# Gates repeated over the partitions by matmuls, one DMA transposition per chunk, x moved by chunk, and a new order: one layer with sliding attention and a gated MLP

## The chip, the cores and the metric

The kernel runs on one core of one Trainium2 chip. The metric is the device time of an execution in microseconds (us); the kernel before is given as the median of three executions. The profile shows one more execution, whose own time is given beside its span (first to last instruction). Engines are named as in the profile: PE is TensorE, DVE is VectorE, ACT is ScalarE, POOL is GpSimd, SP is SyncE (here it only issues DMAs).

## The reference, cut to what matters

One transformer layer, conditioned by a vector c, over 2048 tokens of 640 features, in bfloat16:

```
mod = silu(c) @ w_mod                       # six vectors of 640: sa, ca, ga, sb, cb, gb
h = layernorm(x) * (1 + ca) + sa
q, k, v = split(h @ wqkv)                   # 32 heads of 20
p = softmax(q k^T / sqrt(20), causal, the last 256 keys only)
x = x + ga * ((p v) @ wo)                   # ga: the first gate
h = layernorm(x) * (1 + cb) + sb
x = x + gb * ((sigmoid(h @ w_gate) * (h @ w_up)) @ w_down)    # gb: the second gate; inner width 1536
```

## The kernel before, in words

**Tiling.** The tokens are cut into 8 chunks (`a`) of 256, each of two blocks (`bi`) of 128 tokens, one token per partition. The kernel first computes `mod` (lines 537 to 690), then for each chunk: layer norm 1 (`ln1`), projections (`qkv`), attention, output projection (`outproj`, with layer norm 2), MLP (`mlp`). Weights stay in SBUF; w_mod comes in pieces into the space that wd, wu and hh use later.

**The order is written out by hand.** Every step is an `Op` made by `P.op` (called `A`): engines that may run it, a function, what it reads and writes. `PLAN` (line 295) is a list of integers that gives the order and the engine of each: `code // 5` is the number of the operation in the order of its creation, `code % 5` is its engine in the list PE, ACT, DVE, POOL, SP. `SLOTS` gives, in the same order, which buffer of its pool each tile takes. `emit` writes each engine's instructions in that order, with semaphore waits for what an operation depends on. So each engine works strictly in order: an operation whose input is late holds up all behind it on its engine. That holds for SP too, which issues nearly all DMAs. The costs and priorities in the calls are those of the planner that made `PLAN`; the kernel itself does not use them.

**mod.** `silubc` is silu(c). Five products on TensorE (tags modA, lines 673 to 683), one for each piece of w_mod, give sa and ca into `mA`, copied from PSUM by DVE at line 685. Before and between them stand matmuls on zeros ("warm", `zeros`, line 589; `HEAT` and `REHEAT` count them). The other four vectors come from `mod_tiles` (line 632): a product that leaves the 640 values of a gate as four rows of 160, on the partition groups 0, 32, 64 and 96. `mod_gate` (line 652) scales them into `grow`, writes the four rows to DRAM, and reads them back as one row of 640, repeated over the 128 partitions, into `gbc`. wo (line 1153) and wd (line 1090) are then multiplied by `gbc`, the gate folded into the weight.

**Layer norm and transposition.** `ln_stats` computes mean and variance of each block on DVE (line 700), the power -1/2 on POOL (706, 708), and the normalised block on DVE or POOL (721, 718). The product needs features on the partitions. For chunks 0 and 1 TensorE transposes (`by_block`, `pe_transposes`); for the others, and always for the MLP's input h2T, a DMA transposition from SBUF to SBUF, issued on SP (`transp_dma`, line 728), one per block. `modulate` (line 737) then applies (1 + c) and s to the transposed tile, feature by feature, on DVE, ACT or POOL.

**Projections and attention.** Q and K are evicted to `stg` in groups of 32 columns per head and transposed by DMA per block (by TensorE for chunk 0). A score set (line 916) is 8 or 16 matmuls into four PSUM banks (tile S); ACT takes the exp of the whole set in one instruction (line 943), POOL masks it (951, 953), and the PV product follows (`burst`). There are 6 sets for chunk 0 and 12 for each other chunk, 90 in all. S has one buffer, so the next set waits for the exp. Between the sets, `PLAN` puts projections of later chunks and MLP work of earlier ones on TensorE (all through `mm`, lines 605 and 606, called from `pe_chain`). The projections and the MLP use the pool M of four PSUM banks.

**Loads and stores.** x is loaded in blocks of 128 tokens, once for layer norm 1 (`p_x0`; the first three chunks keep it, `p_x1`) and once more for the residual of the later chunks. The result is stored per block, from SP or ACT.

Of the kernel before, what the change touches and what calls it, by code (L numbers as in the profile page):

```python
# [72 lines left out]

class Op:
# [4 lines left out]
class Prog:  # L79
# [8 lines left out]
    def op(self, eng, fn, dur, reads=(), writes=(), prio=50.0, lat=0.05, work=None, tmin=0.0, extra=(), tag="", hold=(),  # L88
# [41 lines left out]
        for t in hold:  # L130
            tiles[t] = 1
# [159 lines left out]
def c_pe(n):  # L291
# [121 lines left out]
PQ = ()  # L413
KEEP = 3
DSAFE = 1.0
NPB = 0
OUTE = ("sp", "act")
XE = ("sp", "act")
MW = 64
AFTER = 1  # L420
NOW = 1
LEAD = 2
HEAT = (5, 1, 1, 1)
REHEAT = (2, 1, 1, 1, 2)
WSE = (("dve", "pool"), ("dve", "pool"))
# [782 lines left out]
```

## Time and profile before

| | us |
|---|---|
| median of three executions | 332.96 (332.66 to 333.0) |
| the profiled execution's own time | 332.18 |
| its span | 330.4 |
| busy: PE, ACT, DVE, POOL | 320.4, 231.6, 197.9, 180.9 |
| mean granted clock of TensorE | 0.995 |

How to read it: a row of the timeline gives the start, the time that it covers, the engine, the line, the operation with its tiles (out<-in) and a count; brackets give the idle time of the engine before it and what ended it. SPq is a DMA issue on SP: its time is that of the issue, not of the transfer. Groups by line add up busy time (us) and give the mean of one in ns. A row of windows gives, after the stretch and its length, the busy time of PE, PEld (weight loads), DVE, ACT and POOL with their counts, then the granted clock of TensorE as a share of full speed, the DMA engines' share, and GB/s. Matmuls are pipelined, so the time between two starts is the price of one, not its busy time.

### The profile page before, as it was taken

What the parts mean: (1) busy time and instruction counts of PE and PEld (TensorE: products, weight loads), DVE (VectorE), ACT (ScalarE), POOL (GpSimd) and SP (SyncE); (2) the same over time, 40 slices, a digit from 0 to 9 for tenths busy, and PEclk for the clock granted to TensorE, in tenths of its full rate; (3) what the DMA queues carried; (4) which work ended last, traced back from release to release, by engine and by line L of the source; (5) the groups of instructions that cost most, each with busy time, mean ns of one, the idle gap of its engine ahead of it and who ended that gap; (6) DMA issues with size and microseconds to landing.
All of it is one profiled execution on the core that took longest, in us unless ns stands there. A gap on an engine that the chain in (4) does not pass through costs nothing.

```text
span 330.4 us, 9903 instructions
## 1 busy us (share of the span) xinstructions
PE 320.4 (97%) x4115; PEld 228.0 (69%) x4115; DVE 197.9 (60%) x421; ACT 231.6 (70%) x225; POOL 180.9 (55%) x278
## 2 busy tenths in 40 slices
PE   6999999889999999999999999999999999999997
PEld 2676656556676777666776676776776777788885
DVE  4497789466785667665636552565546463584423
ACT  2599788797887787868897977787895777412220
POOL 3246859676768856748573674647382738401000
PEclk9899999999999999999999999999999999999999
DMA  7989999989900662224600500190120002003101
GB/s 236 365 285 219 200 223 190 245 195 284 265 15 13 139 105 40 58 43 108 114 2 22 93 2 2 50 152 17 43 62 22 22 22 62 4 18 59 62 3 41
DMA packets 65719, 33.87 MB, mean 103 GB/s; under 512 B 49930, under 2 KB 64138, under 8 KB 65674
## 3 DMA queue, kind: packets, MB, share of 16 engines
q1 hardware_dynamic: 64368, 31.77, 43.0%
q10 hardware_dynamic: 1306, 1.48, 1.6%
q8 instruction: 32, 0.52, 0.7%
q14 instruction: 13, 0.11, 0.1%
HBM read 18.68 MB, written 2.62 MB: 64 GB/s over the span
## 4 chain that ended last, share of the span: by engine, by line
PE 78%; DMA 9%; POOL 4%; ACT 3%; issue 2%; DVE 2%; SPq 1%; ACTq 0%; POOLq 0%; DVEq 0%
PE M L605 64%; PE S L606 7%; PE M L606 6%; DMA hT<-x 3%; ACT E L943 3%; DMA wu<-in_B_w_up_dram 2%; DMA wd<-in_B_w_down_dram 2%; DMA wd<-in_w_mod_dram 2%; SPq L508 1%; POOL E L951 1%; POOL E L953 1%; POOL hT L737 1%; PE S L605 1%; POOL st L708 0%; DVE hT L757 0%
## 5 line engine op out<-in xcount | busy, mean ns | idle before, releaser
L943 ACT ACTIVATE E<-S 128x2048 bf16<-128x2048 f32 x90 | 168.9, 1877 | 38.8 <-PE S L606 35.8
L951 POOL TENSOR_SCALAR_AFFINE_SELECT E<-E 128x512 bf16<-128x512 bf16 (+2 forms) x90 | 74.2, 836 | 37.6 <-ACT E L943 17.8
L953 POOL TENSOR_SCALAR_AFFINE_SELECT E<-E 128x512 bf16<-128x512 bf16 (+1 forms) x84 | 65.1, 786 | 28.2 <-ACT E L943 13.6
L605 PE MATMUL M<-h2T,wu 128*128 128x256 bf16 x480 | 75.5, 273 | 0.1
L605 PE MATMUL M<-h2T,wg 128*128 128x256 bf16 x480 | 73.7, 273 | 0.0
L605 PE MATMUL M<-wd,hh 128*128 128x320 bf16 (+2 forms) x396 | 59.8, 295 | 0.0
L1109 DVE SCALAR_TENSOR_TENSOR hh<-sig,M 128x512 bf16<-128x512 f32 x48 | 32.3, 677 | 35.7 <-ACT sig L1107 19.0
L605 PEld LDWEIGHTS M<-h2T,wu 128*128 128x128 bf16 x480 | 44.6, 98 | 11.4 <-issue 3.0
L605 PEld LDWEIGHTS M<-h2T,wg 128*128 128x128 bf16 x480 | 45.1, 98 | 9.7 <-issue 1.9
L1107 ACT ACTIVATE sig<-M 128x512 f32<-128x512 f32 x48 | 28.6, 596 | 31.8 <-PE M L605 27.5
L605 PEld LDWEIGHTS M<-wd,hh 128*128 128x128 bf16 x396 | 37.0, 98 | 14.5 <-issue 1.5
L606 PE MATMUL S<-QT,KT 20*128 20x256 bf16 (+1 forms) x960 | 35.9, 245 | 2.3 <-ACT E L943 2.1
L700 DVE BATCH_NORM_STATS2 st<-x 128x6 f32<-128x320 bf16 x64 | 29.1, 476 | 1.3 <-DMA x<-in_A_x_dram 1.0
L605 PE MATMUL M<-wq,hT 128*128 128x320 bf16 x160 | 29.1, 300 | 0.7 <-DVE stg L823 0.4
L606 PEld LDWEIGHTS S<-QT,KT 20*128 20x128 bf16 x960 | 14.1, 92 | 22.1 <-ACT E L943 12.5
L989 DVE STREAM_TRANSPOSE T<-M 128x512 f32<-128x512 f32 x32 | 21.9, 702 | 11.1 <-PE S L606 8.8
L605 PE MATMUL M<-wo,oT 128*128 128x320 bf16 x160 | 28.4, 300 | 0.0
L605 PE MATMUL M<-wv,hT 128*128 128x320 bf16 x160 | 28.3, 299 | 0.1
L605 PE MATMUL M<-wk,hT 128*128 128x320 bf16 x160 | 27.0, 299 | 1.0 <-POOL hT L737 1.0
L1128 DVE TENSOR_TENSOR x<-M,x 128x320 bf16<-128x320 f32 (+2 forms) x33 | 15.6, 476 | 19.9 <-PE M L605 19.5
L823 DVE CAST stg<-M 128x320 bf16<-128x320 f32 x37 | 17.7, 480 | 13.4 <-PE M L605 13.0
L1062 DVE TENSOR_TENSOR x<-M,x 128x320 bf16<-128x320 f32 x32 | 15.3, 484 | 13.7 <-PE M L605 11.6
(78 smaller groups left out, 300.8 us busy)
## 6 DMA issues: line engine op xcount, KB each, us to landing
x<-in_A_x_dram SPq DMA_DIRECT2D x21, 160.0 KB, 3.2
wd<-in_w_mod_dram SPq DMA_DIRECT2D x6, 320.0 KB, 5.1
wd<-in_B_w_down_dram SPq DMA_DIRECT2D x4, 480.0 KB, 6.1
out_dram<-x SPq DMA_DIRECT2D x11, 160.0 KB, 2.0
wu<-in_w_mod_dram SPq DMA_DIRECT2D x5, 320.0 KB, 6.9
wu<-in_B_w_up_dram SPq DMA_DIRECT2D x2, 576.0 KB, 7.7
wg<-in_B_w_gate_dram SPq DMA_DIRECT2D x2, 576.0 KB, 4.6
wq<-in_A_wqkv_dram SPq DMA_DIRECT2D x2, 400.0 KB, 7.6
```

The lines of the kernel that those rows point to most:

```text
L605: return e.matmul(o, l, r, start=st, stop=sp, skip_group_check=True)
L606: return e.matmul(o, l, r, start=st, stop=sp, tile_position=tp, skip_group_check=True)
L700: A("dve", lambda e, g, bi=bi, j=j: e.bn_stats(v(bi * 12 + j * 6, 6), src[bi].ap[:, j * 320:(j + 1) * 320]), 0.48, reads=[src[bi].r()], wr ...
L823: return e.tensor_copy(dst(), src())
L943: A("act", lambda e, eng: e.activation(E.ap[:], Sp.ap[:], ACT.Exp, scale=SM_SCALE), 1.876, reads=[Sp.r()], writes=[E.r()], prio=3, tag=f"e ...
L951: return e.affine_select(ap, ap, pattern=[[0, ap.shape[1]], [1, 128]], compare_op=ALU.is_ge, fill=0.0, base=0, channel_multiplier=-1)
L953: return e.affine_select(ap, ap, pattern=[[0, ap.shape[1]], [-1, 128]], compare_op=ALU.is_ge, fill=0.0, base=-1, channel_multiplier=1)
L989: A("dve", lambda e, g, h=h: e.transpose(T1.ap[:, 512 * h:512 * h + 512], X[h].ap), 0.694, reads=[X[h].r()], writes=[T1.r(h)], prio=3.5, t ...
L1062: A("dve", lambda e, g, ps=ps, bi=bi, half=half: e.tensor_tensor(x1[bi].ap[:, half * 320:half * 320 + 320], ps.ap[:, 0:320], x1[bi].ap[:, ...
L1107: A("act", lambda e, g, pg=pg, sg=sg: e.activation(sg.ap[:], pg.ap[:], ACT.Tanh, scale=0.5), c_act(512), reads=[pg.r()], writes=[sg.r()], ...
L1109: A("dve", lambda e, g, pu=pu, sg=sg, f0=f0: e.scalar_tensor_tensor(out=hh.ap[:, f0:f0 + 2, :], in0=sg.ap[:].rearrange("p (a b) -> p a b", ...
L1128: A("dve", lambda e, g, ps=ps, bi=bi, c0=c0, n=n: e.tensor_tensor(x1[bi].ap[:, c0:c0 + n], ps.ap[:, 0:n], x1[bi].ap[:, c0:c0 + n], op=ALU. ...
```

## The change

- **Gates.** `mod_gate` no longer goes through DRAM: four matmuls multiply a column of the identity matrix, repeated 128 times, with `grow`, which repeats each of the four rows over all partitions in PSUM; two evictions copy the halves to `gbc`.
- **Layout by chunk.** x0, x2, x1, hT, h2T, stg, QT and KT become tiles of a whole chunk with the block as an outer index ([128, 2, ...]); `Half` is the view of one block. Operands that spanned 256 contiguous columns are now two runs of 128.
- **One DMA transposition per chunk** for hT and h2T, instead of two. Q and K keep one per block (`QM` is empty).
- **x loaded, and the result stored, by chunk** (x of chunk 0 and the last chunk's result still by block); the second part of w_mod in two DMAs instead of five (`WM1`).
- **A new PLAN and new SLOTS.** PLAN has 1978 operations instead of 2012; SP has 92 instead of 128, ACT 220 instead of 234, DVE 440 instead of 421, POOL 261 instead of 266.

The new order at the start: SP issues x of chunk 1, x of chunk 0, the five pieces of w_mod for modA, wq, wk, x of chunk 2, wv, x of chunk 3, one part of wo, w_mod's second part and w_gate's first, and then the transposition hT of chunk 2. DVE does the statistics and normalisation of chunks 0 and 1 before it copies mA. On TensorE the heating matmuls stand in a row behind the transposition of c, a transposition of chunk 0 stands before the first modA product and two more before the third; two transpositions of chunk 1 come before the first projection.

```diff
+class Half:
+    def __init__(self, tile, bi):
+        self.tile = tile
+        self.bi = bi
+    def r(self, key=None):
+        return self.tile.r(("b", self.bi, key))
+    @property
+    def ap(self):
+        return self.tile.ap[:, self.bi, :]
...
+WM1 = (3, 5)
+QM = ()
...
-    p_x0 = sbpool("x0", 4, [128, D])
-    p_x2 = sbpool("x2", 2, [128, D])
-    p_x1 = sbpool("x1", 6, [128, D])
-    p_hT = sbpool("hT", 2, [128, NDT, CH])
-    p_h2 = sbpool("h2T", 2, [128, NDT, CH])
-    p_stg = sbpool("stg", 4, [128, 1024])
-    p_QT = sbpool("QT", 3, [128, NG, CH])
-    p_KT = sbpool("KT", 4, [128, NG, CH])
+    p_x0 = sbpool("x0", 2, [128, 2, D])
+    p_x2 = sbpool("x2", 1, [128, 2, D])
+    p_x1 = sbpool("x1", 3, [128, 2, D])
+    p_hT = sbpool("hT", 2, [128, 2, NDT, 128])
+    p_h2 = sbpool("h2T", 2, [128, 2, NDT, 128])
+    p_stg = sbpool("stg", 2, [128, 2, 1024])
+    p_QT = sbpool("QT", 3, [128, 2, NG, 128])
+    p_KT = sbpool("KT", 4, [128, 2, NG, 128])
...
-    def mod_gate(ps, n, factor, prio):
-        g = dram(f"gate{prio}", [4, 160])
-        Rd = R("gdram")
+    def mod_gate(ps, n, factor):
         A("dve", lambda e, _: e.tensor_scalar(grow[:], ps.ap[:, n * 160:n * 160 + 160], factor, None, op0=ALU.mult),
           c_dve(160), reads=[ps.r()], writes=[R_grow], prio=8, tag="grow")
-        dma(lambda: g, lambda: grow[0:128:32, :], 0.05, reads=[R_grow], writes=[Rd], prio=1, tag="gout", dur=0.42)
-        dma(lambda: gbc[:], lambda: g.rearrange("(o a) b -> o (a b)", o=1).to_broadcast([128, D]), 0.45, reads=[Rd], writes=[R_gbc],
-            prio=1, tag="gin", dlat=2.6)
+        gs = [Tile(p_M, "gb") for _ in range(2)]
+        def fn(e, g):
+            for j in range(4):
+                ins = mm(e, gs[j // 2].ap[:, j % 2 * 160:j % 2 * 160 + 160], ident[:, 32 * j:32 * j + 1].to_broadcast([128, 128]), grow[:],
+                         True, True)
+            return ins
+        A("pe", fn, 0.3, reads=[R_grow, R_ident], writes=[t.r() for t in gs], prio=8, lat=0.2, tag="gb", mode=0)
+        for h in range(2):
+            evac(lambda h=h: gbc[:, 320 * h:320 * h + 320], lambda t=gs[h]: t.ap[:, 0:320], 320, [gs[h].r()], [R_gbc[h]], 8, "gbe")
...
-                ap = dst.ap[:, dt, :]
+                ap = dst.ap[:, :, dt, :]
...
-            turned[a] = [transp_dma(lambda bi=bi: t.ap[:, :, bi * 128:(bi + 1) * 128], lambda bi=bi: src[bi].ap[:], 4, 0.29,
-                                    [src[bi].r()], [t.r(("t", bi))], 1.42, f"atr{a}") for bi in range(2)]
+            turned[a] = [transp_dma(lambda: flat3(t), lambda: flat(xt), 4, 0.58, [s.r() for s in src], [t.r("t")], 1.35, f"atr{a}")]
...
-            for bi in range(2):
-                transp_dma(lambda bi=bi: h2.ap[:, :, bi * 128:(bi + 1) * 128], lambda bi=bi: x2[bi].ap[:], 2, 0.29,
-                           [x2[bi].r()], [h2.r(("t", bi))], 1.42, f"btr{a}")
+            transp_dma(lambda: flat3(h2), lambda: flat(x2t), 2, 0.58, [x.r() for x in x2], [h2.r("t")], 1.35, f"btr{a}")
...
+            if a < NCH - 1:
+                if bi == 1:
+                    stored[a] = [dma(lambda: out_flat[2 * a * 128:(2 * a + 2) * 128, :].rearrange("(b p) d -> p b d", p=128), lambda: x1[0].tile.ap[:], 0.84,
+                                     reads=[x.r() for x in x1], prio=10, tag="out", dur=0.45, eng=OUTE)]
```

More of the change, by code (lines that the diff above doesn't have):

```diff
@@ L630, in pe_chain, with evac @@
         return o
+    def evac(dst, src, n, reads, writes, prio, tag):
+        def fn(e, g):
+            if g == "act":
+                return e.activation(dst(), src(), ACT.Copy)
+            return e.tensor_copy(dst(), src())
+        return A(("act", "dve"), fn, {"act": c_act(n), "dve": c_dve(n)}, reads=reads, writes=writes, prio=prio, tag=tag)
     def mod_tiles(parts, prio):
@@ L737, in mo @@
                 return e.tensor_scalar(ap, ap, sc[:, dt:dt + 1], sh[:, dt:dt + 1], op0=ALU.mult, op1=ALU.add)
-            A(MOE, mo, {"dve": 0.34, "act": 0.59, "pool": 0.55}, port=True, reads=[dst.r(("t", bi)) for bi in range(2)] + Rmod, writes=[dst.r(dt)], prio=prio, tag=f"{ln}modu{a}")
+            A(MOE, mo, {"dve": 0.34, "act": 0.59, "pool": 0.55}, port=True, reads=[dst.r("t")] + Rmod, writes=[dst.r(dt)], prio=prio, tag=f"{ln}modu{a}")
     def pe_transposes(src, dst, sc, sh, Rmod, prio, a, ln="a"):
@@ L1046, in outproj @@
         if a < KEEP:
-            x1 = [keep[2 * a], keep[2 * a + 1]]
+            x1 = keep[a]
         else:
-            x1 = [load_x(p_x1, 2 * a + bi, 15, eng=XE, extra=stored.get(a - 3, ())) for bi in range(2)]
+            x1 = load_x(p_x1, a, 15, eng=XE, extra=stored.get(a - 3, ()), tag="y")
         for bi in range(2):
@@ L1067, in outproj @@
                 add_pair(x1[bi], pss, 4.5, f"res1_{a}")
-        x2 = [Tile(p_x2, f"x2_{2 * a + bi}") for bi in range(2)]
+        x2t = Tile(p_x2, f"x2_{a}")
+        x2 = [Half(x2t, bi) for bi in range(2)]
         ln_stats(x1, x2, 7, "b", a)
```

133 lines of the change are left out of this document (69 added, 64 removed), and 208 rows, old and new, of the table PLAN.

## The prediction

> **What bounds the kernel now.** The page comes first: span, engine shares, bytes per slice, the chain that ended last.
>
> ```profile
> span 330.4 us, 9903 instructions
> PE 320.4 (97%) x4115; PEld 228.0 (69%) x4115; DVE 197.9 (60%) x421; ACT 231.6 (70%) x225; POOL 180.9 (55%) x278
> GB/s 236 365 285 219 200 223 190 245 195 284 265 15 13 139 105 40 58 43 108 114 2 22 93 2 2 50 152 17 43 62 22 22 22 62 4 18 59 62 3 41
> PE 78%; DMA 9%; POOL 4%; ACT 3%; issue 2%; DVE 2%; SPq 1%; ACTq 0%; POOLq 0%; DVEq 0%
> ```
>
> TensorE is bound almost throughout, so a change off its queue pays only where TensorE waits. The DMA engines carry 190 to 365 GB/s in the first eleven slices of 8.26 us (to 91 us) and little afterwards. DMA, POOL and ACT stand in the chain at the front; late in the kernel it is TensorE. The change is decided before 91 us.
>
> Next the timeline of TensorE, for unit prices.
>
> ```profile
> 12.64 3.09 PE L605 MATMUL M<-wq,hT 128*128 128x320 bf16 x20 [0.33 <-POOL hT L782]
> ...
> 29.67 0.87 PE L606 MATMUL M<-wu,silubc 128*32 128x160 bf16 x40
> ...
> 33.33 2.21 PE L605 MATMUL M<-wk,hT 128*128 128x320 bf16 x15 [1.01 <-POOL hT L737]
> ...
> 53.42 1.50 PE L606 MATMUL M<-E,V 128*32 128x256 bf16 x64
> 54.85 0.40 PE L606 MATMUL S<-QT,KT 20*128 20x256 bf16 x8
> ...
> 62.28 0.40 PE L606 MATMUL S<-QT,KT 20*128 20x256 bf16 x8
> 62.61 0.45 PE L605 MATMUL M<-wv,hT 128*128 128x320 bf16 x2
> 62.89 0.84 PE L605 MATMUL M<-wk,hT 128*128 128x320 bf16 x5
> 63.57 1.25 PE L605 MATMUL M<-wv,hT 128*128 128x320 bf16 x8
> 66.96 0.40 PE L606 MATMUL S<-QT,KT 20*128 20x128 bf16 x16 [2.14 <-ACT E L943]
> ```
>
> From start to start, five 320-column matmuls take 63.57 - 62.89 = 0.68 us, 0.136 each; a score set 62.61 - 62.28 = 0.33; a PV burst 54.85 - 53.42 = 1.43 (half that for chunk 0). Real projections begin at 12.64.
>
> Then ScalarE's timeline: each score set is followed by one exp.
>
> ```profile
> 19.61 1.88 ACT L943 ACTIVATE E<-S 128x2048 bf16<-128x2048 f32 x1 [0.21 <-PE S L606]
> ...
> 32.37 1.88 ACT L943 ACTIVATE E<-S 128x2048 bf16<-128x2048 f32 x1
> ...
> 36.15 1.88 ACT L943 ACTIVATE E<-S 128x2048 bf16<-128x2048 f32 x1 [0.54 <-PE S L606]
> ...
> 60.26 1.88 ACT L943 ACTIVATE E<-S 128x2048 bf16<-128x2048 f32 x1
> 64.44 0.60 ACT L736 ACTIVATE hT<-hT,mA 128x256 bf16<-128x256 bf16 x1 [2.31 <-DMA hT<-x]
> ...
> 65.05 1.85 ACT L943 ACTIVATE E<-S 128x2048 bf16<-128x2048 f32 x1
> ...
> 69.99 1.88 ACT L943 ACTIVATE E<-S 128x2048 bf16<-128x2048 f32 x1 [0.18 <-PE S L606]
> ```
>
> From the first exp (19.61) to that of chunk 2's first set (69.99) pass 50.4 us. The order list in the code puts there, on TensorE, 235 matmuls of 320 columns (235 x 0.136 = 32.0), 18 score sets (5.9), three PV bursts (0.7 + 0.7 + 1.4), two modulation products of at most 0.87 (1.7) and 28 identity products of 128 columns (by columns 0.055 each, 1.5): 43.9 us. The excess is 6.5. A set costs about 0.1 beyond its work even in an undisturbed stretch (32.37 to 36.15 apart), so 18 x 0.1 = 1.8 is ordinary and **4.7 us are stalls** that an order could avoid. Two are big: 36.15 - 32.37 = 3.78 where the order gives 15 matmuls and a set, 2.4 us with the 0.1 still out (1.3 lost: K of chunk 2 waited for hT); and 65.05 - 60.26 = 4.79 for the same 2.4 (2.3 lost: ScalarE, in order, sat before the modulation of hT of chunk 4, with two exps' work behind it, and TensorE waited 2.14 for the exp). The remaining 1.1 is spread thin. The second stall begins at a DMA transposition:
>
> ```profile
> 56.15 1.13 SPq L508 DMA_DIRECT2D wg<-in_B_w_gate_dram  x2
> 57.39 2.96 SPq L728 DMA_TRANSPOSE hT<-x  x2
> ```
>
> The pair was issued right behind two bulk loads of w_gate; its modulation could start at 64.44, 7 us after 57.39.
>
> **The change, part by part.** *Gates.* Rows by line and shape, then of the DMA view (median us to landing last).
>
> ```profile
> L605 PE MATMUL M<-ident,stg 128*128 128x128 bf16 x32 | 3.1, 219 | 0.0
> ...
> L1153 DVE TENSOR_TENSOR wo<-wo,gbc 128x640 bf16<-128x640 bf16 x5 | 2.1, 478 | 0.9 <-DMA gbc<-gate 0.9
> ...
> L655 DVE TENSOR_SCALAR grow<-M 128x160 bf16<-128x160 f32 x2 | 0.6, 296 | 0.0
> ```
>
> ```profile
> gbc<-gate SPq DMA_DIRECT2D x2, 160.0 KB, 5.1
> h2T<-x SPq DMA_TRANSPOSE x16, 2.6
> QT<-stg SPq DMA_TRANSPOSE x14, 3.4
> ```
>
> Removed: two DMAs per gate and a 5.1 us landing. Only 0.9 us of DVE idleness came from it, off the path. Added per gate: four matmuls of 160 columns, not in the trace; they lie between half of four 320-column ones (0.27) and four identity products of 128 columns with their drain (4 x 3.1/32 = 0.39). I take 0.27, since they stand in a row with other matmuls: 0.55 us for both gates. They lie on TensorE's own queue, with nothing to hide them. Two evictions of 320 columns, about as long as a scaling of wo (0.48), replace the landing; the order puts them on DVE, where they stand beside projections. The product waits for grow; behind it on TensorE stand chunk 1's V projections and the next score sets. grow follows the PV burst and the modulation product, both over a score set earlier, some 4 us of TensorE work, against 0.3 us on DVE and two PSUM transpositions ahead of it: no wait. Two of the four PSUM banks are held until the evictions: zero to 0.5, I take zero.
>
> *One transposition per chunk* (hT, h2T: 28 become 14).
>
> ```profile
> L728 SPq DMA_TRANSPOSE h2T<-x x16: 1199/1228/2100, 67.8 to 303.8; - x16
> L728 SPq DMA_TRANSPOSE QT<-stg x14: 1231/1264/3679, 27.5 to 220.1; - x14
> ```
>
> 640 columns cost SP 1.23 us and 1024 cost 1.26, so the issue hardly depends on size: 14 x 1.23 = 17 us less of SP time, all of it on a queue that ends nothing by itself. Landing: 2.6 us for 640 columns and 3.4 for 1024 gives about 3.9 for 1280; a pair of today lands 1.2 + 2.6 = 3.8 after its first issue (bounds: 2.6, as if size were free, and 2 x 2.6 = 5.2). So nothing is gained where both halves are ready, and where the second is late the merged one lands 1.3 later after it (2.6 to 3.9). Behind it on SP wait the next loads and q/k transpositions. After 91 us TensorE has work of other chunks to cover 1.3 us; before, it is in the stalls below. The two-run operands (2 x 128 columns) I price at nothing: the modulation product reads one of its weights in five runs of 32 columns and takes the same time per matmul.
>
> *Loads and stores by chunk* save SP issues of about 0.4 us each, again beside other work; a store then waits for the second half, which reuse of its buffer two chunks later covers.
>
> *The new order, head.* SP now issues chunk 1's x, then x of chunk 0, and only then w_mod; DVE does both chunks' statistics before it copies mA.
>
> ```profile
> 4.84 0.87 DVE L700 BATCH_NORM_STATS2 st<-x 128x6 f32<-128x320 bf16 x2
> ...
> 8.45 0.45 DVE L721 TENSOR_SCALAR x<-x,st 128x640 bf16<-128x640 bf16 x1 [1.02 <-POOL st L708]
> ...
> 11.69 0.17 DVE L685 COPY mA<-S 128x10 f32<-128x10 f32 x1 [2.79 <-PE S L605]
> ```
>
> ```profile
> 5.35 0.60 PE L592 MATMUL S<-E 128*128 128x512 bf16 x2
> ...
> 9.09 0.74 PE L605 MATMUL S<-silubc,wd 128*128 128x64 bf16 x10
> ...
> 10.05 0.74 PE L605 MATMUL S<-silubc,wd 128*128 128x64 bf16 x10
> ```
>
> ```profile
> 8.00:9.00 1.00, 1.00 (x14) 0.72 (x12) 0.45 (x1) 0.03 (x1) 0.41 (x1) 0.50 0.97 325
> ...
> 11.00:12.00 1.00, 1.00 (x18) 0.80 (x16) 0.31 (x3) 0.04 (x1) 0.00 (x0) 0.86 1.11 373
> ```
>
> DVE from 4.84: eight statistics (8 x 0.435), four aggregations (about 0.2), four normalisations (0.45), two memsets (0.2) make 6.5 us, so mA at 11.4, and with a wait for POOL's powers 11.9 instead of 11.69: **+0.2**. The w_mod pieces come 320 KB later, 1.0 us at the 325 GB/s of the window from 8 to 9, and TensorE waits longer than that for DVE. So TensorE is the question. Its first transposition now stands ahead of all five w_mod products and needs a normalisation that DVE reaches at about 7.9, and another one needed before the third product ends at 9.9. Today's products run at a granted clock of 0.50 (window 8 to 9), one with its reheating every 10.05 - 9.09 = 0.96 us. From 7.9 at that pace, with the transpositions, mA would come at 13.2: **+1.5**. But the new order runs its eight heating matmuls in one piece right before that point, where today they are done, in pieces, at 5.35 + 0.60 = 5.95 and TensorE then stands; those last two took 0.30 each, and half the clock came after the standstill. I take the full clock as granted: +0.2, and keep +1.5 as a rival.
>
> The Trainium skill, "TensorE: Matmul & The Clock Gate", section "Part 1: The HAM clock gate", says that the clock opens after a window of about 3.4 us of sustained work, and that the window runs freely. By that rule eight matmuls of heat just suffice, and run by run they may not; the 0.50 of the windows agrees with a gate of two states.
>
> *The new order, front.* Counted in the lists: up to chunk 2's first set TensorE has 5 projections fewer, and two transpositions have moved under the head (-0.2). K of chunk 2 comes after a score set more of other work, and no load blocks SP before hT of chunk 2: the 1.3 us stall goes. The wo scalings come earlier on DVE: half of the spread 1.1 goes. For chunk 4 the w_gate loads now stand behind hT. But the second K transposition of chunk 1, issued soon after that chunk's first exp (36.15 today), blocks SP till about 37, and behind it ten bulk loads, 4.2 MB, and five q/k and one hT transposition (1.6 MB) stand ahead of hT: 5.8 MB at the 223 to 245 GB/s of the busy slices after 40 us is 24 to 26 us, so it lands, itself included, at 62 to 65; at the bulk rate of 365 it would be 55. ScalarE reaches the modulation at about 60 (the exp before it, 60.26 today, comes some 1.5 earlier and lasts 1.88). I take 62, a stall of 2, and half of the spread waits: 2.6 of the 4.7 remain.
>
> **Sum.** One more wait counts, from the list of waits:
>
> ```profile
> PEld M L605 <- DMA wu<-in_B_w_up_dram: 0.4, 1, 0.4
> ```
>
> Against the profiled run (332.18; span 330.4, and 1.8 around it): +0.2 head, +0.55 gates, -0.2 transpositions moved, -4.7 + 2.6 stalls = -1.55, and -0.4 for the wait on the last w_up load after 80 us, which is issued some places earlier in the new order: about -2.0. The median of the runs shown, 332.96, lies 0.78 higher; against it, **331.0**.
>
> **Rivals.**
> 1. *The front runs clean*: hT of chunk 4 lands by 60, as the bulk rate would allow; stalls 0.6 instead of 2.6: 329.0. For it: SP issues fewer commands; against it: the bytes above.
> 2. *Cold head*: the clock is 0.5 during the w_mod products, +1.5 instead of +0.2: 332.3. For it, the 0.50 of the windows; against it, heat in one piece.
> 3. *The bulk holds hT of chunk 4* (slower): at 223 GB/s or less hT lands at 65; ScalarE stands 5 us before an exp and TensorE with it: +3 on the forecast, 334.0. It turns the sign from a landing of about 64 (331.0 + 2). For it: 7 us of latency today; against it: w_gate no longer stands before it and the gates' trip has gone.
> 4. *Nothing changes*: other waits take the place of those removed; 332.3 to 333.6. The forecast bets on half of them.
>
> **Chances.** About 0.2% (0.7 us) is what a measurement of this kernel can tell from no change. Forecast 0.40 (329.8 to 332.2), clean 0.18, cold 0.12 (half of it faster), slower 0.20, nothing 0.10. Faster 0.64, same 0.16, slower 0.20. The range leaves out half of the clean case's far side and of the slow one's: 328.3 to 334.2; the likeliest case's own is 329.8 to 332.2.
>
> **What would show it.** Head: first projection at 12.6 to 13.0 with a clock of 1.0 from 8 to 12 (14 and 0.5: rival 2). Front: exps of chunk 1's first set no more than 2.6 us behind the one before. ScalarE's wait before hT of chunk 4: about 2 us; none is rival 1, over 4 is rival 3. Gates: eight matmuls, under 0.6 us. Wrong altogether if TensorE's stalls after 91 us change, where I expect none.

## The result, and the profile after

The change made the kernel **slower by 0.67%**: 334.05 us (median of 15 executions, 332.32 to 335.54) against 332.04 for the kernel before, run beside it (15 executions, 330.1 to 333.0); ratio 1.0067, 95% interval 1.0042 to 1.0092. The forecast was 331.0. The profiled execution took 334.05 us, its span is 332.3 (before 330.4). Ratios here leave disturbed executions out, so they differ a little from the quotients of the medians.

The page of the changed kernel: span, engines, GB/s in 40 slices, the chain that ended last.

```profile
span 332.3 us, 9821 instructions
PE 320.7 (97%) x4123; PEld 229.0 (69%) x4123; DVE 201.8 (61%) x440; ACT 227.0 (68%) x215; POOL 183.0 (55%) x273
GB/s 233 370 373 141 221 248 214 202 216 290 166 62 36 8 73 136 3 82 80 121 49 2 38 5 2 41 145 0 73 113 2 41 2 42 41 0 65 17 41 39
PE 87%; DMA 9%; SPq 1%; ACT 1%; DVE 1%; issue 0%; DVEq 0%
```

The busy shares hardly differ from those before. What tells the two apart is ScalarE's timeline, the starts of the exps:

```profile
18.64 1.88 ACT L975 ACTIVATE E<-S 128x2048 bf16<-128x2048 f32 x1 [0.21 <-PE S L626]
...
31.18 1.88 ACT L975 ACTIVATE E<-S 128x2048 bf16<-128x2048 f32 x1
33.65 1.88 ACT L975 ACTIVATE E<-S 128x2048 bf16<-128x2048 f32 x1
...
55.10 1.88 ACT L975 ACTIVATE E<-S 128x2048 bf16<-128x2048 f32 x1 [0.51 <-PE S L626]
59.45 0.44 ACT L655 ACTIVATE stg<-M 128x320 bf16<-128x320 f32 x1 [2.47 <-PE M L625]
61.31 0.44 ACT L655 ACTIVATE stg<-M 128x320 bf16<-128x320 f32 x1 [1.43 <-PE M L625]
61.78 1.88 ACT L975 ACTIVATE E<-S 128x2048 bf16<-128x2048 f32 x1
63.55 0.59 ACT L768 ACTIVATE hT<-hT,mA 128x256 bf16<-128x256 bf16 x1
...
66.72 1.88 ACT L975 ACTIVATE E<-S 128x2048 bf16<-128x2048 f32 x1 [0.27 <-PE S L626]
...
71.39 1.88 ACT L975 ACTIVATE E<-S 128x2048 bf16<-128x2048 f32 x1 [2.69 <-PE S L626]
```

The first exp (the first score set of chunk 0) is 0.97 us earlier than in the profile before (19.61), and the stall in front of chunk 1's first set is gone (33.65 - 31.18 = 2.47, before 3.78). Then come two new ones, where the order gives a plain set of 2.5 us: 61.78 - 55.10 = 6.68 (**4.2 lost**) and 71.39 - 66.72 = 4.67 (**2.2 lost**). The stall of before at the modulation of hT of chunk 4 is gone: ScalarE comes to it at 63.55 without waiting. Over the span: -0.97 to the first exp, +3.69 from there to chunk 3's first exp (91.56 against 87.87; 1.2 of it is TensorE work that the order moved in there, by the prediction's unit prices), -0.82 after it, which makes +1.9 in all.

What ended the two new waits, from the chain of waits between 50 and 75 us (start, length, what):

```profile
50.47 5.91 DMA x<-in_A_x_dram
...
56.41 0.04 DVE st L732
...
57.29 0.63 DVE T L1021
...
57.97 3.31 PE M L625 x12
61.28 0.44 PE S L626 x8
...
61.78 7.35 DMA QT<-stg
...
69.22 1.79 PE M L625 x12
```

First wait: the load of chunk 5's x was issued at 50.47 and took 5.91 us. VectorE stood before chunk 5's statistics for it; behind those, in order, stood the turn of the PV result (T, line 1021) that frees a PSUM bank, and TensorE's next projection wanted that bank. Second wait: TensorE stood 2.03 us for Q3's transposition, though nobody wanted chunk 3's Q yet. The projection wanted was chunk 4's Q, and its staging buffer `stg` was still being read. (A projection reserves its staging buffer when it starts.) SP's timeline shows why both were late:

```profile
44.48 5.87 SPq L760 DMA_TRANSPOSE QT<-stg  x2
50.47 0.51 SPq L524 DMA_DIRECT2D x<-in_A_x_dram  x1
51.04 0.46 SPq L524 DMA_DIRECT2D wu<-in_B_w_up_dram  x1
51.66 5.87 SPq L760 DMA_TRANSPOSE KT<-stg  x2
57.64 1.36 SPq L760 DMA_TRANSPOSE hT<-x  x1
59.05 1.22 SPq L524 DMA_DIRECT2D wg<-in_B_w_gate_dram  x2
60.44 6.58 SPq L760 DMA_TRANSPOSE QT<-stg  x2
```

A transposition of Q or K is issued in 1.23 to 1.26 us when little is in flight; here two take 5.87 (Q2, and again K2) and 6.58 (Q3). Bulk loads stand in front of each pair; that they are the reason is tested below. Not every issue behind a load stretches: of K2's two the first takes 1.24 and the second 4.58, of Q3's 1.24 and 5.24. hT of chunk 3, behind four loads, took 9.7 us from issue to landing. All that follows on SP shifts with them. The Trainium skill, "Perfetto Trace Analysis", section "DMA Instruction — HWDGE (DVE, Sync)", says that the span shown of such an issue includes the wait for the descriptor generator and the writing of all descriptors, and that the DMA engines may begin early when these overfill the buffer. The rows agree with that reading: what stretches is the issue (5.24 us for one), not only the transfer.

The waits were 2.41 and 2.03 us, but the first one cost 4.2. TensorE's windows behind it (granted clock third from last):

```profile
58.00:60.00 2.00, 2.00 (x8) 1.13 (x9) 2.00 (x7) 0.44 (x1) 0.00 (x0) 0.52 1.23 253
60.00:62.00 2.00, 2.00 (x16) 0.87 (x15) 0.59 (x2) 0.66 (x2) 0.44 (x1) 0.63 1.02 183
```

The clock fell to half after the standstill: 4 us at 0.52 and 0.63 lose 1.7, and 2.4 + 1.7 is nearly all of the stall.

### The profile page after: what moved, and what is told of

Same layout as the page of the kernel before. It is cut to its first block, busy times and chain, and to the rows that moved or that the text cites. A ratio compares the mean times of both kernels' runs of the same rounds, so it can differ in the third digit from the quotient of the medians.

```text
span 332.3 us, 9821 instructions
## 1 busy us (share of the span) xinstructions
PE 320.7 (97%) x4123; PEld 229.0 (69%) x4123; DVE 201.8 (61%) x440; ACT 227.0 (68%) x215; POOL 183.0 (55%) x273
## 3 DMA queue, kind: packets, MB, share of 16 engines
HBM read 18.35 MB, written 2.62 MB: 63 GB/s over the span
## 4 chain that ended last, share of the span: by engine, by line
PE 87%; DMA 9%; SPq 1%; ACT 1%; DVE 1%; issue 0%; DVEq 0%
PE M L625 73%; PE S L626 8%; PE M L626 6%; DMA hT<-x 3%; DMA QT<-stg 2%; DMA wd<-in_w_mod_dram 2%; DMA x<-in_A_x_dram 2%; SPq L524 1%; ACT E L975 1%; SPq L760 0%; DVE T L1021 0%; ACT hT L768 0%; DVE hT L814 0%; DVE st L732 0%; PE S L625 0%
## 5 line engine op out<-in xcount | busy, mean ns | idle before, releaser
L985 POOL TENSOR_SCALAR_AFFINE_SELECT E<-E 128x512 bf16<-128x512 bf16 (+1 forms) x84 | 67.1, 809 | 47.2 <-ACT E L975 36.4
L625 PE MATMUL M<-h2T,wu 128*128 128x256 bf16 x480 | 74.3, 273 | 0.0
L625 PE MATMUL M<-h2T,wg 128*128 128x256 bf16 x480 | 72.9, 273 | 0.0
L625 PE MATMUL M<-wd,hh 128*128 128x320 bf16 (+2 forms) x396 | 60.5, 295 | 0.0
L625 PEld LDWEIGHTS M<-h2T,wu 128*128 128x128 bf16 x480 | 45.5, 98 | 9.7 <-issue 1.9
L656 DVE CAST stg<-M 128x320 bf16<-128x320 f32 x43 | 20.5, 482 | 17.4 <-PE M L625 17.2
L625 PE MATMUL M<-wv,hT 128*128 128x320 bf16 x160 | 29.0, 302 | 0.0
L625 PE MATMUL M<-wk,hT 128*128 128x320 bf16 x160 | 28.3, 300 | 0.1
L1021 DVE STREAM_TRANSPOSE T<-M 128x512 f32<-128x512 f32 x32 | 21.6, 699 | 10.1 <-PE S L626 9.7
L625 PE MATMUL M<-wo,oT 128*128 128x320 bf16 x160 | 27.4, 299 | 0.0
```

The costliest lines, as they stand in the source:

```text
L625: return e.matmul(o, l, r, start=st, stop=sp, skip_group_check=True)
L656: return e.tensor_copy(dst(), src())
L985: return e.affine_select(ap, ap, pattern=[[0, ap.shape[1]], [-1, 128]], compare_op=ALU.is_ge, fill=0.0, base=-1, channel_multiplier=1)
L1021: A("dve", lambda e, g, h=h: e.transpose(T1.ap[:, 512 * h:512 * h + 512], X[h].ap), 0.694, reads=[X[h].r()], writes=[T1.r(h)], prio=3.5, t ...
```

## The experiments

Theory **transfers**: bulk loads among the transpositions in SP's order delay these and x. Rival theory **order**: VectorE's order (chunk 5's statistics in front of T) made it. Rival theory **staging**: buffers by chunk make a projection wait for two transpositions. Apart from these three, the gates and the head are tried by themselves. In SP's orders below, T q2.0 is the transposition of block 0 of chunk 2's Q, x5 the load of chunk 5's x; wu0.1 is w_up's first half of columns, second part (parts .0 576 KB, .1 384 KB), wg w_gate alike; wm are parts of w_mod, wd of w_down. "Stretch" is the time from the first exp to that of chunk 3's first set, "first exp" its start, both of one profiled execution, which need not be a typical one. Each median stands beside that of the kernel before, run with it, and only the ratios compare across rows.

| kernel | median us | before beside it | ratio (95%) | first exp | stretch |
|---|---|---|---|---|---|
| changed kernel | 334.05 | 332.04 | 1.0067 (1.0042 to 1.0092) | 18.64 | 91.56 |
| stats_later | 334.39 | 332.01 | 1.0077 (1.0045 to 1.0108) | 18.84 | 91.00 |
| bulk_later | 332.48 | 332.01 | 1.0038 (1.0009 to 1.0068) | 19.26 | 89.20 |
| stats_and_bulk | 332.52 | 332.01 | 1.0018 (0.9988 to 1.0049) | 18.62 | 89.17 |
| before_pe_gates | 332.93 | 332.01 | 1.0018 (0.9981 to 1.0055) | 18.03 | 89.90 |
| burst_in_before | 335.93 | 332.57 | 1.0105 (1.0064 to 1.0146) | 18.41 | 89.46 |
| stats_and_staging | 332.83 | 332.57 | 0.9998 (0.9967 to 1.003) | 20.03 | 90.06 |
| staging_by_block | 332.61 | 332.57 | 1.0016 (0.998 to 1.0051) | 19.76 | 91.01 |
| all_mended | 335.01 | 332.57 | 1.0075 (1.0043 to 1.0106) | 20.43 | 93.28 |
| mended_short_q3 | 332.73 | 331.95 | 1.0003 (0.9974 to 1.0032) | 19.14 | 88.61 |
| mended | 330.74 | 331.95 | 0.9972 (0.9935 to 1.0009) | 20.38 | 88.50 |
| x_first_in_before | 334.56 | 331.95 | 1.007 (1.0038 to 1.0102) | 20.45 | 87.27 |
| mended_and_head | 336.80 | 331.95 | 1.0138 (1.0102 to 1.0174) | 18.37 | 93.72 |
| head_back | 337.13 | 332.65 | 1.0122 (1.0073 to 1.017) | 19.14 | 94.20 |
| mended_2 | 330.65 | 332.65 | 0.9937 (0.9902 to 0.9972) | 18.74 | 86.69 |
| mended_2_head | 334.06 | 332.65 | 1.0039 (1.0008 to 1.007) | 19.28 | 91.96 |
| order_only | 331.19 | 333.31 | 0.9942 (0.9908 to 0.9976) | 19.99 | 87.57 |
| order_and_stats | 331.01 | 333.31 | 0.9938 (0.9908 to 0.9967) | 19.52 | 87.58 |

**stats_later**: VectorE's order alone.

```diff
 DVE: ... T of chunk 1,
-stats 5.11, stats 5.10, T, evict q3.11, mt, grow, stats 5.00, evict q3.00, ...
+T, evict q3.11, mt, grow, evict q3.00, stats 5.11, 5.10, 5.00, ...
```

> The changed kernel with one thing moved: the three statistics of chunk 5 that VectorE does first (they wait for x of chunk 5) stand behind the eviction of chunk 3's Q instead of in front of the turn of the heads' result (T<-M), whose PSUM bank the next projections want. Theory order (the order on VectorE made the loss): the 4.3 us between the exps of sets 1.12 and 1.13 falls under 0.5, the 2.3 us before the first exp of chunk 2 was only its echo, and the kernel comes to about 328 us. Theory transfers (SP's queue made it: bulk loads among the transpositions stretch their issues, 5.9 us for the two of Q2, 5.9 for those of K2, 6.6 for those of Q3): hT of chunk 4 still lands at about 61 and Q3 at about 67 to 69, TensorE that comes 4 us earlier waits for those instead, and no more than 1.5 us is won: 332.5 to 334.

Nothing won. The first stall went and came back as others, from TensorE's timeline of this run:

```profile
58.52 0.70 PE L625 MATMUL M<-wk,hT 128*128 128x320 bf16 x4 [0.85 <-DMA KT<-stg]
67.38 3.17 PE L625 MATMUL M<-wq,hT 128*128 128x320 bf16 x12 [3.57 <-DMA QT<-stg]
```

Both are projections waiting for a transposition that still reads their staging buffer; behind the second one the clock halved again. So VectorE's order did not make the loss: with it mended, TensorE only met the next tile that was late.

**bulk_later** and **stats_and_bulk**: only SP's order; then both.

```diff
 SP: wo.0, x4,
-wu1.0, wm2.1, wu0.1, wm3.0, T hT3, wm3.1, wm2.0, T q2.0, T q2.1, x5, wu0.0, T k2.0, T k2.1, T hT4, wg1.0, wg0.1, T q3.0, ...
+wm2.1, wm3.0, T hT3, wm3.1, wm2.0, T q2.0, T q2.1, x5, T k2.0, T k2.1, wu0.0, T hT4, wg0.1, wu0.1, T q3.0, ...
+(wg1.0 behind T k3.0; x6 and wu1.0 behind T q4.0)
```

> The changed kernel with five bulk loads of SP's queue moved back and nothing else: the three pieces of w_up that stand before and between the transpositions of hT3, Q2 and K2, and the first w_gate piece of the second half, go behind the transpositions of K2, hT4 and K3. Theory transfers: Q2's two issues take about 2.5 us instead of 5.9, x of chunk 5 is issued at 46 to 48 instead of 50.5 and lands by 52, both stalls (4.3 and 2.3 us) fall under 1 us each, and the kernel comes to 328 to 329.5 us. Theory order: x comes earlier too, so the first stall shrinks all the same, but the second one stays as far as it isn't an echo. If neither holds and the loads don't stretch the issues, these stay over 5 us for two and the time stays at 334.

> Both moves together. Theory transfers: like the bulk loads alone, 328 to 329 us, the order adds under 0.5. Theory order: like the order alone, about 328. If the two are separate limits that each hold the other up, only this one falls below 330 while either alone stays above 331.

In bulk_later Q2's two issues took 3.03 us instead of 5.87:

```profile
45.11 3.03 SPq L760 DMA_TRANSPOSE QT<-stg  x2
```

x of chunk 5 was issued at 48.26 and landed in 3.5 us, and the first stall went with VectorE's order untouched. The stretch fell by 2.4 in both, which speaks for transfers. The time did not fall to the 328 to 329.5 that was expected: about 1.8 stayed in front of chunk 2 (Q3, behind wu0.0, wg0.1 and wu0.1), and some 1.3 came at 87 us (the last w_down part landed 9.4 and 9.5 us after its issue).

**burst_in_before**: the same cause put into the kernel before.

```diff
 SP: ... x9, wu0.0,
-T hT3.0, ...
+wu1.0, wu0.1, T hT3.0, ...
```

> The kernel before with two bulk loads of w_up (960 KB together) moved ahead, in front of the first transposition of hT3, where the changed kernel has them; nothing else differs, so everything else that the change does is absent. Theory transfers (bulk loads in front of the transpositions make the loss): the issues of hT3 and of the transpositions behind it stretch, chunk 2's and 3's Q and K come later, and the kernel before loses 1 to 3 us: 333 to 335. If the loss needs the changed kernel's own shape (chunk-wide transpositions, chunk-wide staging buffers), it stays at 332.

Slower by 1.05%, and 1.6 us in the stretch (89.46 against 87.87). So the two loads cost time without any of the change. But the issues behind them stretched little here (from SP's timelines: the second of hT3 2.54 us against 2.27, the first of K2 1.94 against 1.32), so this run shows the price of loads that are moved ahead and not by which path it is paid. The rest of the 3.4 us isn't in this profile (332.54, where the median is 335.93) and stays open.

**before_pe_gates**: the gates alone, in the kernel before.

```diff
-grow -> DRAM -> gbc (two DMAs per gate)
+four matmuls behind chunk 1's V projection (second gate: behind a score set), two VectorE evictions
```

> The kernel before with the gates alone changed: the two gate rows repeated over the partitions by four TensorE instructions and two VectorE evictions each, no write to DRAM and no broadcast load; all else, its order too, as before. My step: TensorE work of under 0.6 us in all, hidden in part, 332.0 to 332.6 us against 332.0. Rival, the gates are what costs the change its time (banks of PSUM held, VectorE late with its evictions): 334 or more. The other rival, the trip through DRAM held something up: 331 or less.

No change in time that can be measured. Where I had put the first pair of evictions, TensorE waited for a bank, a price that the prediction had put at nothing:

```profile
33.35 3.87 PE L606 MATMUL M<-wk,hT 128*128 128x320 bf16 x15 [2.12 <-DVE gbc L829]
```

15 matmuls in 3.87 us instead of some 2.2: the clock halved here too, and the stretch is 2.0 longer than before's; the first exp of this execution came 1.6 earlier (mA at 9.85 instead of 11.69). In the changed kernel the gates stand elsewhere, and no such row is there.

**stats_and_staging**, **staging_by_block**: staging buffers by block again, in the same memory.

```diff
-p_stg = sbpool("stg", 2, [128, 2, 1024])
+p_stg = sbpool("stg", 4, [128, 1024])
```

> The changed kernel with chunk 5's statistics behind the eviction, as before, and with the staging buffers of Q and K by block again (four of 128x1024 in place of two of 128x2x1024, the same memory; the transpositions were by block all along). With the order alone TensorE stood 1.1 us for K2's transposition and 5.4 us for Q3's, each time in front of a projection whose staging buffer was being read. Theory staging (a projection has to wait for both transpositions of a chunk where it waited for one): both waits fall by more than half and the kernel comes to 331 or less. Theory transfers: the two transpositions of a pair land about 1 us apart, so about 1 us each is won: 332.5 to 333.5.

> The changed kernel with only the staging buffers by block again. Theory staging: the 2.3 us before the first exp of chunk 2 (TensorE waits for Q3's transposition, which still reads the buffer that chunk 4's Q wants) go for the greater part, the 4.3 us of the first stall stay: 332 to 332.5. Theory transfers: the pair lands 1 us apart under the load, and 1 us is won at most: 333 to 334.

Their ratios are 0.5% (staging_by_block against the changed kernel) and 0.8% (stats_and_staging against stats_later) lower. In stats_and_staging the wait before chunk 4's Q shrank from 3.57 to 2.47 us: the first of the two transpositions lands earlier, no more. In staging_by_block's profile that wait is 2.22 us, where the changed kernel has 2.03 (TensorE came to it without the first stall), and the clock halved behind it (6.44 us to chunk 2's first exp); x of chunk 5, issued in the same place of SP's order, landed there in 3.91 us, so the first stall nearly went (0.41 us of waiting). So the size of each stall differs from execution to execution, and staging has at most a share, as long as the transfers are late.

**all_mended**, **mended_short_q3**, **mended**, **mended_2**: both moves, staging by block, and four orders of SP from T hT4 on.

```diff
 all_mended:      wg0.1, wu0.1, T q3.0, T q3.1, T h2T0, T k3.1, wd1, T k3.0, wd2, T q4.0, x6, wd3, wd0, wg1.0, wu1.0, wg1.1, wu1.1, T hT5
 mended:          wg0.1, wu0.1, T q3.0, T q3.1, T h2T0, T k3.1, wd1, T k3.0, wg1.0, wd2, T q4.0, wd3, x6, wd0, T hT5, wu1.0, T k4.0, wg1.1, wu1.1
 mended_short_q3: T q3.0, T q3.1, wg0.1, wu0.1, T h2T0, T k3.1, wd1, T k3.0, wd2, wg1.0, T q4.0, wd3, wd0, T hT5, x6, wu1.0, T k4.0, wg1.1, wu1.1
 mended_2:        T q3.0, T q3.1, wg0.1, wu0.1, T h2T0, T k3.1, wd1, T k3.0, wd2, wg1.0, T q4.0, wd3, wu1.0, T hT5, x6, wg1.1, wu1.1, T k4.0, wd0
```

> The changed kernel with all of it together: the statistics behind the eviction, the w_up and w_gate loads behind the transpositions, the staging buffers by block, and the four loads of w_down put ahead of the second half's w_gate and w_up (in the run with both moves VectorE waited for the last of them until 85.3 us, and TensorE lost 1.35 us there). Against that run, 332.5: the 1.9 us in front of chunk 2 fall by about 1 and the 1.35 us go, so 329.5 to 330.5, under both kernels. If these waits only hand on to the next one, as the order alone did, 332 or more.

> The changed kernel with the statistics behind the eviction, the staging buffers by block, w_up's three loads and w_gate's one behind the transpositions, and two things otherwise than in the run with all of it: Q3's transpositions ahead of the second pieces of w_gate and w_up, and hT5's ahead of most of the second half's loads (there hT5 took 9.9 us to land behind four bulk loads, which cost TensorE 7 us in two sets). Theory transfers: the wait before chunk 2 falls under 1 us, that at hT5 goes; against 332.0 for the kernel before, 329.5 to 331. If it only hands the wait on to the w_gate and w_up pieces that the MLP of chunk 0 wants at 75 us, 332 or more.

> As the run before this one, but with the second pieces of w_gate and w_up left in front of Q3's transpositions, as in the run with both moves. Theory transfers: the wait before chunk 2 stays at 1 to 2 us, w_down and hT5 are in time, and the kernel comes to 330 to 331.5. If the DMA queues are so full between 34 and 90 us that any order loses the same, 332 to 334.

> The run mended_short_q3 (statistics behind the eviction, staging by block, bulk loads behind the transpositions, Q3's first) with the first half of w_up's second columns in front of hT5's transposition, where SyncE stood idle for 3 us, the second halves in front of K4's, and the last w_down piece, with its scaling, later. There TensorE lost 2.1 us at 88 us waiting for w_up. Theory transfers: those go, nothing else is late, and the time falls from 332.7 by 1.5 to 2: 330.5 to 331.2. If the wait hands on to hT5 or w_down, 332 or more.

all_mended handed the loss on: six bulk loads stand in a row in front of T hT5, whose landing took 9.86 us; POOL stood 4.25 us for it with the masks of chunk 2 behind, TensorE 3.71 for POOL. With Q3's transpositions in front of wg0.1 and wu0.1 (mended_short_q3) the stall before chunk 2 went; w_up was then late at 88 us (1.89 us), and mended_2 mended that by loading w_up in the 3 us in which SP stood idle before T hT5. mended_2 is faster than the kernel before by 0.63% (0.28 to 0.98).

**order_only**, **order_and_stats**: mended_2's SP order with staging by chunk, and with VectorE's statistics as in the changed kernel or behind the eviction. One scaling of w_down moves back with the load that it waits for; nothing else differs.

> The changed kernel with nothing but SyncE's order (and the scaling of wd's first part, which goes with it) as in mended_2: staging buffers by chunk and chunk 5's statistics stay as changed. mended_2 was 1.3% under the changed kernel. Theory transfers alone: the order gives all of it, 330.5 to 331.3. Theory that the staging buffers have a share of their own: the projections of chunk 4's Q wait for both transpositions of Q3, 0.5 to 1.5 us more than there: 331.3 to 332.5.

> The same with the statistics behind the eviction: mended_2 with the staging buffers by chunk. If those buffers matter once the transfers are in order, 0.5 to 1.5 us above mended_2 (331.2 to 332.3), with TensorE's wait on Q3's transposition back in front of chunk 4's Q; if not, the same as mended_2 within 0.5.

Both have mended_2's ratio. SP's order alone (with that scaling), the change else as it was, turns +0.67% into -0.58%. order_only's SP timeline, and then ScalarE's:

```profile
45.83 3.12 SPq L760 DMA_TRANSPOSE QT<-stg  x2
49.07 0.51 SPq L524 DMA_DIRECT2D x<-in_A_x_dram  x1
49.75 4.96 SPq L760 DMA_TRANSPOSE KT<-stg  x2
54.76 0.57 SPq L524 DMA_DIRECT2D wu<-in_B_w_up_dram  x1
55.43 1.34 SPq L760 DMA_TRANSPOSE hT<-x  x1
58.29 3.40 SPq L760 DMA_TRANSPOSE QT<-stg  x2
```

```profile
58.48 1.88 ACT L975 ACTIVATE E<-S 128x2048 bf16<-128x2048 f32 x1
62.12 0.60 ACT L768 ACTIVATE hT<-hT,mA 128x256 bf16<-128x256 bf16 x1 [1.76 <-DMA hT<-x]
62.63 1.85 ACT L975 ACTIVATE E<-S 128x2048 bf16<-128x2048 f32 x1
64.39 0.43 ACT L655 ACTIVATE stg<-M 128x320 bf16<-128x320 f32 x1
65.52 1.88 ACT L975 ACTIVATE E<-S 128x2048 bf16<-128x2048 f32 x1 [0.71 <-PE S L626]
...
68.00 1.88 ACT L975 ACTIVATE E<-S 128x2048 bf16<-128x2048 f32 x1 [0.50 <-PE S L626]
```

(The 4.96 of K2 holds a wait for its second eviction: the two issues are 1.24 and 1.68.) This is the picture that the prediction drew, in another order: hT of chunk 4 lands at 62.1, ScalarE waits 1.76 for it, and nothing else of size is late. With the same 43.1 us of work, 68.00 - 19.99 = 48.0 leaves 3.1 us of stalls, where the prediction had 2.6.

**The head**: x_first_in_before, mended_and_head, head_back, mended_2_head.

```diff
 x_first_in_before, SP:
+x3, x2,
 wm0.0, x1, x0, wm0.2, wm0.1, wm0.3, wm0.4, wq0, wq1,
-x3, x2,
 ...
 head_back, SP (x of chunk 1):
-x1, x0b, x0a, wm0.0 to wm0.4, wq1, ...
+x0b, x0a, wm0.0 to wm0.4, x1, wq1, ...
 (its statistics behind chunk 0's Q, its TensorE transpositions behind chunk 0's K)
```

> The kernel before with one move in the head: the two loads of chunk 1's x (320 KB) go in front of w_mod's first pieces and chunk 0's x, where the changed kernel has them. In the executions of the kernel before whose clock stayed at 1.00 the copy of mA came at 9.8 and 9.9 us, in the changed kernel's at 10.9. Theory load order (320 KB at some 360 GB/s in front of w_mod are that difference): the copy of mA comes at 10.6 to 10.9 at clock 1.00, and the time rises by about 0.9, to 333 to 333.5. If the load order costs nothing, 9.8 to 9.9 and 332.0 to 332.6. The difference that the clock makes in the head (11.7 at 0.50 to 0.68) blurs both.

> As the run before this one, with chunk 1's x loaded behind the first two pieces of w_qkv instead of ahead of all else, and chunk 1's statistics, normalization and its five TensorE transpositions moved behind chunk 0's Q. Theory load order: the copy of mA comes at 9.8 to 10.0 instead of 10.9 and the first exp 0.8 to 1.0 us earlier; if nothing of chunk 1 becomes late by it, the time is 0.8 to 1 under that run. If the head isn't bound by the landing of w_mod's pieces, no difference.

> The changed kernel with its head alone put back in order: chunk 1's x is loaded behind w_mod's first five pieces instead of ahead of everything, its statistics and normalization follow chunk 0's Q on VectorE, and its five TensorE transpositions follow chunk 0's K. The rest, the stalls at 57 and 67 us included, stays as changed. Theory load order: the copy of mA comes at 9.9 to 10.2 instead of 10.9, the first exp about 0.8 us earlier, and the time falls by 0.8 to 2 (the same move cost the kernel before 0.7%): 332 to 333.3. If the head isn't where the rest of the loss is: 334 and no less. If chunk 1 becomes late, as when its x was loaded behind two pieces of w_qkv, a stall shows between the first exps of chunk 0.

> Both of the two runs before this one together. If the head and the middle are two separate losses, their gains add: 329 to 330.3, under the kernel before. If only one of them is a loss, as that one alone.

Chunk 1's x in front cost the kernel before 0.7%. What its profiled execution lost (332.63, 1.9 below its median) lies before the first exp (20.45; its stretch is no longer than before's); the rest of the 0.7% is not in this profile. Its mA came at 12.48, not at 10.6 to 10.9, at a clock of 0.81 and then 0.50, so the load order and the clock are not told apart. Putting x back in the changed kernel brought mA from 10.94 to 10.42 but made chunk 1 late, as its expectation had allowed: TensorE waited up to 0.77 us at a time for evictions, and chunk 0's second and third exp came 4.61 and 3.89 us behind the one before, 2.1 and 1.4 more than in the changed kernel. mended_and_head and mended_2_head, expected to be faster, lost in the same way (mA at 10.41 and 10.66, but 7.18 and 4.61 us from the first exp to the second). From ScalarE's timeline of head_back, its first three exps:

```profile
19.14 1.88 ACT L975 ACTIVATE E<-S 128x2048 bf16<-128x2048 f32 x1 [0.17 <-PE S L626]
...
23.75 1.87 ACT L975 ACTIVATE E<-S 128x2048 bf16<-128x2048 f32 x1
...
27.64 1.88 ACT L975 ACTIVATE E<-S 128x2048 bf16<-128x2048 f32 x1
```

## Why the prediction was wrong, point by point

- **The step that failed: "I take 62, a stall of 2, and half of the spread waits: 2.6 of the 4.7 remain."** Counted in the same way, 18.64 to 71.39 is 52.75 us with 43.1 of work and 1.8 of ordinary set price: **7.8 us** of stalls, not 2.6. The landing itself was right within 1 us: hT of chunk 4 was issued at 57.64 and landed 3.4 later, at 61.1, and ScalarE did not wait for it at all. (In part by luck: the DMA engines carried 237 GB/s from 34.73, where SP came to the bulk, to 61.06, inside the range that was assumed, but SP came there some 2 us earlier than assumed.) What failed was to put the whole price of the bulk on that one tile. Everything behind the bulk on SP is late, and I followed only what had been late in the profile before. Two other tiles made the stalls: x of chunk 5, for which VectorE stood in order (4.2 us lost), and Q3's transposition, through its staging buffer (2.2 lost).
- **Two missing links.** I priced the merged buffers by SP time and landing alone and not by when they are free: a chunk-wide `stg` makes chunk 4's Q wait for both of Q3's transpositions. And a wait that is added must be followed through VectorE's order as I did through ScalarE's. With the transfers in order neither costs anything that can be measured (order_only 0.9942, mended_2 0.9937), so they carry the delay on and do not make it.
- **1.7 us of the first stall were clock.** No term had it: 2.41 us of waiting cost 4.2.
- **Rival 3 named the cause** (bulk in front of hT of chunk 4) and nearly the time (334.0), but not the way: its test, ScalarE over 4 us before the modulation, would have said no, since that wait is none. That its time came so near is luck: it was +1.0 on the 332.96 of the forecast, and measured are +2.0 on 332.04. A rival's test has to name every tile behind the cause.
- **Head, +0.2**: against the profiled execution of before it was -0.75 (mA 11.69 to 10.94), but one execution says little here. Twelve profiles have the changed kernel's head (its own, and those of the experiments that do not touch it). VectorE's work came as forecast: the third normalisation starts at 9.8 to 10.1. mA, however, came anywhere from 10.92 to 12.72, the first exp from 18.62 to 20.43, in two ways that the timeline of TensorE tells apart. The changed kernel, warm and on time:

```profile
8.29 0.46 PE L625 MATMUL S<-silubc,wd 128*128 128x64 bf16 x10
8.58 0.38 PE L612 MATMUL S<-E 128*128 128x512 bf16 x1
```

The same of mended, whose mA came at 12.68:

```profile
9.01 0.74 PE L624 MATMUL S<-silubc,wd 128*128 128x64 bf16 x10
9.56 0.61 PE L611 MATMUL S<-E 128*128 128x512 bf16 x1
```

And of order_only, mA at 12.28:

```profile
9.37 0.47 PE L625 MATMUL S<-silubc,wd 128*128 128x64 bf16 x10 [1.05 <-DMA wd<-in_w_mod_dram]
```

In mended the products take as long as in the profile before at a granted clock of 0.50 (0.74, and 0.61 for a heating matmul): that is **rival 2, the cold head**, at its price (12.68 - 10.94 = 1.7, forecast 1.5 - 0.2 = 1.3), in three executions of twelve (mended, all_mended, stats_and_staging). So "I take the full clock as granted" holds in most executions only. In order_only and four others (bulk_later, mended_short_q3, order_and_stats, staging_by_block) the products run at full speed but the w_mod pieces land late: 6.0 to 6.9 us from issue to landing, against 5.4 to 5.7 in the four that were on time and 4.3 in before_pe_gates (medians of the five pieces): "TensorE waits longer than that for DVE" failed there. Where before's head ran warm, mA came at 9.85 (before_pe_gates, VectorE's timeline) and 9.92 (burst_in_before):

```profile
9.85 0.17 DVE L691 COPY mA<-S 128x10 f32<-128x10 f32 x1 [0.95 <-PE S L606]
```

The means of the first exp are 19.45 over the twelve and 18.68 over the three with before's head (19.61, 18.03, 18.41). On this the new head loses some 0.8 us; with three executions on one side, and no version that mends the head without hurting chunk 1, its size stays open.

- **Gates, +0.55**: right. From the groups by line of the changed kernel: eight matmuls of 0.07 us from start to start (four between 71.27 and 71.55), 0.6 in all, and four evictions of 0.486 (0.48 was assumed).

```profile
L656 DVE CAST gbc<-M 128x320 bf16<-128x320 f32 x4 | 1.9, 486 | 0.7 <-PE M L625 0.7
L625 PE MATMUL M<-grow,ident 128*128 128x160 bf16 x8 | 0.9, 235 | 0.0
```

- **One transposition per chunk**: right in size. In the DMA view of the changed kernel (median us to landing last) h2T by chunk is issued in 1.34 us and lands in 3.4 (median of 8; forecast 3.9; 2.6 for half of it). No run has it alone; order_only, which has it, shows no loss from it. The operands in two runs of 128 columns cost nothing, as assumed: the h2T products take 273 ns on average before and after.

```profile
h2T<-x SPq DMA_TRANSPOSE x8, 3.4
```

- **The stall at chunk 1's first set** went as forecast (2.47, no more than 2.6), the wait of 0.4 us on w_up's last load is gone, as forecast, and after 91 us TensorE's stalls did not change.

## What to carry to other kernels

When loads move ahead on a queue that works in order, as SP does here, list everything that stands behind them, then for each the first engine that meets it and what that engine has behind it; the tile that was late before is only one of them. A merged buffer is free only when the last of its readers is done: ask who wants it next. The version to keep is order_only: the change as it is, with each bulk load just behind the transposition that the next sets need, 331.19 against 333.31 (ratio 0.9942).

## What the runs showed of the hardware

- **A short standstill may halve TensorE's clock.** After waits of 2.41 (changed kernel), 3.57 (stats_later) and 2.12 us (before_pe_gates) it was granted 0.50 for some 3.4 us; after 2.14 (before), 2.03 (changed kernel's second), 2.02 (order_only) and even 2.62 us (burst_in_before) it stayed at 1.00. So the length of the wait alone doesn't decide it. The Trainium skill, "TensorE: Matmul & The Clock Gate", section "Why this matters for your kernels", says to leave no idle gaps above some 3 us between bursts of matmuls; here 2.1 was enough at times, so a wait between 2.1 and 2.6 us had two prices in these runs: its own, or some 1.7 us more.
- **The mean clock of an execution comes in steps of 0.005**, which is 3.4 us at half clock in 331. Of the 125 executions of the kernel before that count in the experiments' ratios, 38 were at 1.000 (mean 331.1 us), 62 at 0.995 (332.4), 25 lower. The changed kernel had 3 of 15 at 1.000, order_only 9 of 12 and stats_and_bulk 12 of 12. So part of what an order wins is clock: from the mean clocks of the two, an estimated 1.1 us of the 4.1 between the changed kernel and order_only. And one profiled execution may be of either kind.
- **The granted clock of a window isn't enough where heat is short.** In mended the window from 9 to 10 us shows 1.00, and the matmuls in it take 0.74 and 0.61 us where warm ones take 0.46 and 0.38 (the clock is third from last):

```profile
9.00:10.00 1.00, 1.00 (x13) 0.72 (x12) 0.26 (x2) 0.00 (x0) 0.77 (x2) 1.00 1.06 346
```

There the duration of a repeated small matmul told more than the window's clock.
- **The issue of a DMA transposition can stretch behind bulk loads**: 1.23 us with little in flight, 2.6 to 5.2 for the stretched ones of the changed kernel (though 1.24 for the first of K2 and of Q3); what follows on the queue starts later by as much.
